# Fused attention and gated convolution on one core: transposes that take turns between two pairs of PSUM banks, a first scores step of its own, and a re-dealt instruction order

## The chip, the cores and the metric

The kernel runs on one core of a Trainium2 chip. The metric is device microseconds of one execution; three runs of the kernel before gave 257.99, 259.13 and 259.63 us, median 259.13 us. The engines are named as the profile names them: PE is TensorE (PEld its weight loads), DVE is VectorE, ACT is ScalarE, POOL is GpSimd, SP is SyncE, which issues the loads and stores.

## The reference

Two stages, the second on the first's output. Four batches, eight heads of width 64, 768 positions; local attention over 96 keys plus 8 global keys, with a linear bias per head.

```python
scores = scale * np.matmul(q, k.transpose(0, 1, 3, 2))
scores = np.where(keep, scores + bias, -1000000000.0)
a = np.exp(scores - np.max(scores, axis=-1, keepdims=True))
a = a / (np.sum(a, axis=-1, keepdims=True) + 1e-09)
x = np.matmul(a, v)                      # all heads side by side: 512 columns
for k in range(5):
    gate_pre += conv_w[k] * xp[:, k:k + S, :]
gate = 1.0 / (1.0 + np.exp(-gate_pre))
out = (gate * (x @ w_val)) @ w_out
```

## The kernel before

**Tiling.** Attention goes by 32 groups (batch, half of the sequence, pair of heads), each of three steps of 128 queries: 96 steps. The second stage goes by eight phases (batch, half), each fed by four groups.

**Operations.** Every operation has a key. For a group g: `L` and `LV` are its loads (SP; group 0's keys and queries come in two parts, `L` 0 and `LB`); `S` all its scores (PE); per step and head `AM` adds the bias and takes the row minimum (DVE), `EX` is the exponential (ACT), `NM` the division by the row sum (POOL, DVE or ACT), with `RG` and `RC` as the guarded reciprocal of a batch of one to three steps; `PT` transposes a batch's probabilities into PSUM (PE), `EV` copies that out in two halves (ACT or DVE), `PV` is the product with the values for a pair of groups (PE), `XS` copies its result out (ACT or DVE). In the second stage `XH` and `XL` split x into a high and a low part, `CV` are the five taps of the convolution, `SG` the tanh, `VM` the product with w_val, `GM` the gate, `GH` and `GL` the split of its result, `OM` the product with w_out, `OE` and `ST` the copy-out and store. `W…` operations decode the 64-bit weights in the first quarter, `BIAS`, `BI2` and `DIST` make the bias tables. `FA`, `FB` and `FC` compute a flag at the end (DVE, PE, DVE).

**Order.** `Plan.add` collects the operations with what each needs; the table `SLOTS` gives each one its place in one list over all engines, and `ENGINES` says which engine does it. The program is emitted in that order, so each engine does its part of the list strictly in order. `plan.ring` adds the dependencies of a buffer that is used in turn.

**PSUM.** Eight banks: two (`pts`) for the transposes, and for the weight sums `WS`; two (`x`) for P.V; two (`s`) for scores; two (`moe`) for `VM` and `OM`. Each `PT` writes both banks of `pts`, so it waits for both `EV` of the `PT` before it.

**Zero products.** `WARM` at the start is 12 products of constants of 512 columns (two of them write `pts`), ahead of the first scores; three blocks `F` of 4, 7 and 6 more stand between the first operations of PE.

Of the kernel before, what the change touches and what calls it, by code (L numbers as in the profile page):

```python
# [16 lines left out]
WARM, FILL_N = 10, (4, 7, 6)  # L17
# [105 lines left out]
    "XH": (
        182, 221, 276, 281, 404, 405, 545, 546, 628, 637, 673, 712, 770, 817, 893, 937, 955, 1010, 1040, 1145, 1164,
        1219, 1249, 1278, 1321, 1361, 1427, 1451, 1509, 1539, 1581, 1608,
    ),
    "XL": (
        191, 229, 284, 285, 468, 538, 554, 569, 647, 766, 767, 780, 826, 850, 962, 965, 989, 1039, 1094, 1175, 1188,
        1222, 1258, 1287, 1325, 1366, 1473, 1477, 1529, 1544, 1597, 1610,
    ),  # L130
# [1042 lines left out]
```

## Time and profile before

| | us |
|---|---|
| median of three runs (lowest, highest) | 259.13 (257.99, 259.63) |
| profiled execution, its own time | 258.13 |
| its span in the trace | 256.3 |
| PE busy | 246.5 |
| DVE busy | 222.4 |
| ACT busy | 193.7 |
| POOL busy | 138.7 |

The span is the time from the first to the last instruction that the profile shows; the time of the same execution is 1.8 us longer. A busy share is a union of instruction times over the whole span; it mixes stretches in which different engines set the pace, so it has to be read stretch by stretch. The end of a matmul is modelled, so PE reads as busy where it only follows closely; what counts for it are the starts of its instructions and the waits listed in front of them.

### The profile page before, as it was taken

The numbers are of one execution on the slowest core, as the hardware profiler recorded it, in microseconds if no ns is written. First come the engines' busy times: TensorE is split into PE (matmuls) and PEld (weight loads), VectorE is DVE, ScalarE is ACT, GpSimd is POOL, SyncE is SP. The second block draws the span as 40 slices with busy tenths as digits, with TensorE's granted clock in tenths as the row PEclk, the third lists the DMA queues.
The fourth block names the chain that finished last, engine by engine and source line by source line (L and its number), as shares of the span: only waits on it lengthen the run. The fifth ranks groups of instructions, "written<-read, shape, count | busy, mean of one in ns | idle before, by whom it ended". The sixth has DMA issues, their size and how long they took to land.

```text
span 256.3 us, 8977 instructions
## 1 busy us (share of the span) xinstructions
PE 246.5 (96%) x3386; PEld 207.5 (81%) x3386; DVE 222.4 (87%) x780; ACT 193.7 (76%) x660; POOL 138.7 (54%) x226
## 2 busy tenths in 40 slices
PE   8989899999999999999999999999999999999983
PEld 3557578788789987999888988898889889889963
DVE  3999999999999999999999889899797797889520
ACT  4989999999989999999897585698966756324011
POOL 4776999999877834344555696154725223140100
PEclk9999999999999999999999999999999999999999
DMA  5969765953256049160628170082012061002112
GB/s 158 379 188 344 245 245 191 391 203 130 63 180 243 17 124 338 56 208 5 226 68 315 69 258 1 8 279 106 6 41 82 4 207 41 0 3 75 47 43 90
DMA packets 16303, 36.37 MB, mean 142 GB/s; under 512 B 1920, under 2 KB 4480, under 8 KB 16256
## 3 DMA queue, kind: packets, MB, share of 16 engines
q1 hardware_dynamic: 16112, 35.75, 40.5%
q8 instruction: 28, 0.46, 0.7%
q14 instruction: 19, 0.16, 0.2%
q10 hardware_dynamic: 144, 0.00, 0.0%
HBM read 29.46 MB, written 6.29 MB: 139 GB/s over the span
## 4 chain that ended last, share of the span: by engine, by line
PE 69%; DVE 21%; ACT 3%; DMA 2%; issue 2%; POOL 1%; SPq 0%; POOLq 0%; DVEq 0%
PE o L859 25%; PE val L836 21%; PE s L624 8%; PE x L709 6%; DVE gate L794 6%; DVE t L632 5%; PE pt L675 5%; PE x L702 3%; DMA kq<-in_kq 2%; ACT p L643 2%; PE warm L406 1%; DVE p L662 1%; DVE ab L299 1%; DVE g L843 1%; DVE rs L654 1%
## 5 line engine op out<-in xcount | busy, mean ns | idle before, releaser
L643 ACT ACTIVATE p<-t,mins 128x168 f32<-128x168 f32 (+1 forms) x192 | 81.2, 427 | 7.8 <-DVE mins L632 3.6
L794 DVE SCALAR_TENSOR_TENSOR gate<-xs,cwt,gate 128x384 f32<-128x384 f32 x128 | 83.0, 664 | 0.8 <-POOL gate L798 0.3
L662 POOL TENSOR_SCALAR p<-p,rs 128x168 f32<-128x168 f32 (+1 forms) x91 | 52.4, 585 | 31.0 <-DVE rs L654 25.3
L632 DVE CUSTOM_DVE_ANT_0 t<-s,bias 128x168 f32<-128x168 f32 (+1 forms) x192 | 54.4, 316 | 3.8 <-PE s L624 3.3
L836 PE MATMUL val<-xh,wvh 128*128 128x384 f32 x128 | 44.9, 351 | 0.5 <-DVE g L843 0.3
L836 PE MATMUL val<-xl,wvh 128*128 128x384 f32 x128 | 43.3, 339 | 0.1
L836 PE MATMUL val<-xh,wvl 128*128 128x384 f32 x128 | 43.2, 338 | 0.0
L850 POOL TENSOR_TENSOR gl<-g,gh 128x384 fp32r<-128x384 f32 x22 | 24.6, 1123 | 29.2 <-DVE gh L299 22.3
L859 PE MATMUL o<-woh,gh 128*128 128x512 f32 (+1 forms) x100 | 40.1, 401 | 0.0
L859 PE MATMUL o<-woh,gl 128*128 128x512 f32 (+1 forms) x100 | 38.6, 386 | 0.9 <-DVE gl L850 0.9
L297 ACT COPY ab<-pt 128x384 f32<-128x384 f32 (+3 forms) x60 | 29.2, 500 | 12.8 <-PE pt L675 12.6
L859 PE MATMUL o<-wol,gh 128*128 128x512 f32 (+1 forms) x100 | 38.6, 386 | 0.0
L624 PEld LDWEIGHTS s<-kq 64*64 64x64 f32 x1088 | 30.9, 133 | 8.6 <-issue 5.6
L643 ACT ACTIVATION_READ_ACCUMULATOR p<-t,mins 128x1 f32 x192 | 37.3, 194 | 0.0
L624 PE MATMUL s<-kq 64*64 64x104 f32 (+3 forms) x1088 | 35.7, 264 | 1.3 <-PE pt L675 0.6
L660 ACT ACTIVATE p<-p,rs 128x168 f32<-128x168 f32 (+1 forms) x68 | 27.9, 428 | 5.2 <-DVE rs L654 5.0
L675 PEld LDWEIGHTS pt<-ident,p 64*104 64x104 f32 (+1 forms) x544 | 19.5, 131 | 9.9 <-issue 3.3
L675 PE MATMUL pt<-ident,p 64*104 64x64 f32 (+1 forms) x544 | 25.3, 226 | 1.8 <-ACT ab L297 1.7
L650 POOL TENSOR_SCALAR sm<-sm 128x4 f32<-128x4 f32 (+2 forms) x31 | 9.2, 296 | 31.2 <-ACT p L643 30.1
L836 PEld LDWEIGHTS val<-xh,wvh 128*128 128x128 f32 x128 | 24.0, 188 | 2.5 <-DVE g L843 0.6
L871 ACT ACTIVATE ob<-o 128x512 f32<-128x512 f32 (+1 forms) x22 | 12.5, 574 | 17.2 <-PE o L859 17.2
L836 PEld LDWEIGHTS val<-xl,wvh 128*128 128x128 f32 x128 | 24.1, 188 | 1.0 <-DVE xl L786 0.3
(157 smaller groups left out, 422.8 us busy)
## 6 DMA issues: line engine op xcount, KB each, us to landing
kq<-in_kq SPq DMA_DIRECT2D x16, 444.0 KB, 5.5
va<-in_va SPq DMA_DIRECT2D x16, 384.0 KB, 4.3
out<-ob SPq DMA_DIRECT2D x24, 256.0 KB, 3.4
kq<-in_kq SPq DMA_DIRECT2D x15, 392.0 KB, 5.7
va<-in_va SPq DMA_DIRECT2D x16, 320.0 KB, 4.5
w<-in_wv SPq DMA_DIRECT2D x8, 256.0 KB, 5.0
w<-in_wo SPq DMA_DIRECT2D x3, 512.0 KB, 4.3
w<-in_wo SPq DMA_DIRECT2D x2, 256.0 KB, 3.5
```

The costliest lines, as they stand in the source:

```text
L297: nc.scalar.copy(dst, src)
L624: nc.tensor.matmul(s[rows, u : u + w], T["rq", g][r, k * P + half * QH : k * P + (half + 1) * QH], T["rk", g][r, c : c + w], start=True, s ...
L632: nc.vector.tensor_tensor_reduce(out=t[:, :n], in0=T["s", s // HB, s % HB, j][:, :n], in1=bias[:, h, :P] if n == P else bias[:, h, P:], op ...
L643: nc.scalar.activation(T["p", s][:, j, :n], T["t", s, j][:, :n], AF.Exp, bias=mins[:, s, j : j + 1], scale=-1.0, accum_out=T["sm", batch_o ...
L660: nc.scalar.mul(pr, pr, rs)
L662: engine(e).tensor_scalar(out=pr, in0=pr, scalar1=rs, scalar2=1.0, op0=ALU.mult, op1=ALU.mult)
L675: nc.tensor.transpose(pts[h][:m, c0 : c0 + QH], pr[rows, c : c + m], ident[rows, rows])
L709: nc.tensor.matmul(T["x", g][rows(i), c0 : c0 + P], T["near", g][:n, k, j], T["a", HB * g + k][:n, j * P : (j + 1) * P], start=False, stop ...
L794: nc.vector.scalar_tensor_tensor(out=gt, in0=src, scalar=w, in1=gt, op0=ALU.mult, op1=ALU.add)
L836: nc.tensor.matmul(T["val", ph, m], (wvh, wvh, wvl)[r][:, m, c * P : (c + 1) * P], (T["xh", g], T["xl", g], T["xh", g])[r], start=(c == 0 ...
L850: engine(e).tensor_sub(tile_of(("gl", ph, m), [P, HT], F32R, "gl", 5), T["g", ph, m], T["gh", ph, m])
L859: nc.tensor.matmul(T[key][:, cols], (T["gh", ph, c], T["gl", ph, c], T["gh", ph, c])[r][:, rows], (woh, woh, wol)[r][:, c, cols], start=(c ...
```

## The change

Four things are changed.

1. The two banks of P.V become fixed tiles `xb`. Within each pair of groups the batches of transposes take turns: the first uses `pts`, the next `xb`, and so on (17 of the 42 batches use `xb`). A `PT` in `xb` needs the `EV` of the earlier `xb` batches of its pair, and the `XS` of the two groups of the pair before.
2. The first step's scores are an operation of their own, `S0`, which needs only the first part of group 0's load; `S` 0 does the other two steps.
3. `WARM` is seven zero products (four of them write the four banks) in place of twelve. The blocks `F` keep their sizes.
4. All places in `SLOTS` and many engines in `ENGINES` are dealt anew.

```diff
-WARM, FILL_N = 10, (4, 7, 6)
+WARM, FILL_N = 3, (4, 7, 6)
...
+    "S0": (8,),
...
-    pts = [psum.tile([P, 4 * P], F32, tag=f"pt{i}", name=f"pt{i}", bufs=1) for i in range(2)]
+    pts, xb = ([psum.tile([P, 4 * P], F32, tag=f"{t}{i}", name=f"{t}{i}", bufs=1) for i in range(2)] for t in ("pt", "x"))
...
+    turns = {}
+    for s in batches:
+        before = [t for t in batches if t // (2 * HB) == s // (2 * HB) and t < s]
+        turns[s] = xb if len(before) % 2 else pts
...
-        for t in (pts if first else []) + [T["warm",]] * n:
+        for t in (pts + xb if first else []) + [T["warm",]] * n:
...
-    def scores(g):
+    def scores(g, ks):
...
-        for k in range(HB):
+        if 0 in ks:
+            for j in range(2):
+                tile_of(("sb", g, j), [P, 4 * P], F32, "s", S_B, psum)
+        for k in ks:
...
-                    nc.tensor.transpose(pts[h][:m, c0 : c0 + QH], pr[rows, c : c + m], ident[rows, rows])
+                    nc.tensor.transpose(to[h][:m, c0 : c0 + QH], pr[rows, c : c + m], ident[rows, rows])
...
-            tile_of(("x", g), [P, HT], F32, "x", X_B, psum)
+            T["x", g] = xb[g % X_B][:, :HT]
...
+    plan.add(("S0",), (PE,), lambda e: scores(0, range(1)), [("L", 0)])
...
-                bank = [d for h in range(2) for d in plan.ring(f"pt{h}", 1, key, [("EV", ss[0], h)])]
+                if turns[s0 := ss[0]] is pts:
+                    bank = [d for h in range(2) for d in plan.ring(f"pt{h}", 1, key, [("EV", s0, h)])]
+                else:
+                    q = s0 // (2 * HB)
+                    bank = [("EV", t, h) for t in batches if t // (2 * HB) == q and t < s0 and turns[t] is xb
+                            for h in range(2)] + [("XS", i) for i in (2 * q - 2, 2 * q - 1) if i >= 0]
```

The new order at three places, read from the two tables:

- PE at the start. Before: `WARM` (12), `S` 0, `F` (4), `S` 1, `PT` 0, `F` (6), `S` 2. After: `WARM` (7), `S0`, `S` 0, `F` (6), `S` 1, `PT` 1, `F` (4), `PT` 0, `S` 2. DVE after `DIST` 1: before two `BIAS`, then the six `AM` of group 0; after one `AM`, one `BIAS`, five `AM`.
- Ahead of `S` 12 (place 477 before, 476 after, with the same operations of PE ahead of it). DVE has 3 `EV`, 2 `XL`, one `BIAS`, `NM`, `RC` and `W2` less, and 2 `GL`, one `GH`, `WH` and `WP` more. POOL has 6 `NM`, 3 `HI`, 2 `BIAS`, one `WA` and `XL` more, and 5 `WH`, one `WP`, `GL` and `RG` less. ACT has 6 `NM`, 2 `EX`, one `BIAS`, `WA` and `XH` less, and 4 `WH`, 3 `EV` and one `GH` more.
- The end. Before, PE: `OM` 84, 85, `FB`, 86, 87, 88, 89; DVE: `GM` 31, `FC`, `GL` 31. After, PE: `OM` 84, 85, `FB`, 86, 88, 89, 87; DVE: `GM` 31, `FC`, with `GL` 31 on POOL. Four taps of group 31 (`CV` 156 to 159) move to a place between `GM` 28 and `GM` 29. Numbers of `OM` count the products of one row block and one quarter of w_out: 84 to 87 are one output block, 88 to 91 the next.

## Rows read from the trace of the kernel before

**Rows 1.** The chain that ended last, by engine (page).

```profile
PE 69%; DVE 21%; ACT 3%; DMA 2%; issue 2%; POOL 1%; SPq 0%; POOLq 0%; DVEq 0%
```

**Rows 2.** Stretches of the span: busy us (x instructions) per engine, granted clock, DMA.

```profile
25.00:60.00 35.00, 33.00 (x614) 27.00 (x606) 34.67 (x132) 34.68 (x124) 33.45 (x49) 1.00 0.69 247
...
92.00:243.60 151.60, 151.52 (x1880) 132.77 (x1877) 134.17 (x422) 107.14 (x348) 64.46 (x96) 1.00 0.32 108
```

**Rows 3.** The chain in order of time near 120 us: start, length, what.

```profile
121.07 0.62 PE pt L675 x16
121.69 1.04 PE s L624 x24
122.73 2.30 PE o L859 x9
```

**Rows 4.** What the transposes (L675) waited for, whole span: us, times.

```profile
  ACT ab L297: 3.3, 6
```

**Rows 5.** Timeline of the first 10 us.

```profile
0.75 1.32 SPq L381 DMA_DIRECT2D kq<-in_kq  x2
...
0.79 1.01 PE L406 MATMUL pt<-const-bfloat16-1.0 128*128 128x512 bf16 x2 [0.79 <-PEq L1163]
1.59 3.84 PE L406 MATMUL warm<-const-bfloat16-1.0 128*128 128x512 bf16 x10
...
5.36 1.02 PE L624 MATMUL s<-kq 64*64 64x128 f32 x32
...
5.56 0.23 DVE L454 TENSOR_SCALAR xs<-xs,counts 128x8 f32<-128x8 f32 x1
...
6.59 0.29 DVE L632 CUSTOM_DVE_ANT_0 t<-s,bias 128x128 f32<-128x128 f32 x1 [0.51 <-PE s L624]
...
7.96 1.31 PE L624 MATMUL s<-kq 64*64 64x128 f32 x32 [0.61 <-DVE mins L632]
...
9.52 1.48 PE L406 MATMUL warm<-const-bfloat16-1.0 128*128 128x512 bf16 x6
```

**Rows 6.** Loads of the first 20 us: issues, KB each, us to landing.

```profile
kq<-in_kq SPq DMA_DIRECT2D x1, 272.0 KB, 3.4
...
kq<-in_kq SPq DMA_DIRECT2D x1, 128.0 KB, 3.1
```

**Rows 7.** Groups by line and shape: busy us, mean ns, idle before.

```profile
L299 DVE COPY ab<-pt 128x384 f32<-128x384 f32 x15 | 8.2, 544 | 0.2 <-PE pt L675 0.2
...
L786 DVE TENSOR_TENSOR xl<-xs,xh 128x384 fp32r<-128x384 f32 x17 | 10.2, 602 | 0.0
...
L850 DVE TENSOR_TENSOR gl<-g,gh 128x384 fp32r<-128x384 f32 x10 | 6.2, 630 | 1.2 <-ACT gh L297 1.2
...
L662 POOL TENSOR_SCALAR p<-p,rs 128x168 f32<-128x168 f32 x74 | 44.1, 603 | 28.5 <-DVE rs L654 23.9 <-ACT p L643 1.8 <-DVE xs L299 1.4
...
L850 POOL TENSOR_TENSOR gl<-g,gh 128x384 fp32r<-128x384 f32 x22 | 24.6, 1123 | 29.2 <-DVE gh L299 22.3 <-ACT gh L297 6.9
...
L299 POOL CAST wvh<-('w', 3)_h 128x512 fp32r<-128x512 f32 x1 | 0.8, 811 | 0.0
...
L299 POOL COPY xs<-xs 128x4 f32<-128x4 f32 x6 | 2.5, 418 | 0.1
...
L297 ACT COPY xs<-x 128x384 f32<-128x384 f32 x26 | 11.9, 468 | 1.7 <-PE x L709 1.7
...
L794 DVE SCALAR_TENSOR_TENSOR gate<-xs,cwt,gate 128x384 f32<-128x384 f32 x128 | 83.0, 664 | 0.8 <-POOL gate L798 0.3
```

**Rows 8.** Timeline of the end.

```profile
243.07 0.51 ACT L297 CAST gh<-g 128x384 fp32r<-128x384 f32 x1 [6.46 <-DVE g L843]
...
244.45 0.39 PE L859 MATMUL o<-woh,gh 128*128 128x512 f32 x1
...
245.11 0.54 DVE L850 TENSOR_TENSOR gl<-g,gh 128x384 fp32r<-128x384 f32 x1
245.70 0.51 PE L859 MATMUL o<-woh,gl 128*128 128x512 f32 x1 [0.86 <-DVE gl L850]
```

More of the change, by code (lines that the diff above doesn't have):

```diff
@@ L25 @@
     "L": (
-        1, 4, 6, 14, 23, 105, 129, 183, 189, 194, 321, 326, 332, 379, 431, 449, 485, 618, 720, 729, 732, 736, 769,
-        825, 935, 1011, 1019, 1024, 1053, 1125, 1229, 1237,
+        1, 4, 6, 11, 26, 105, 140, 186, 190, 198, 263, 303, 348, 359, 440, 502, 506, 600, 616, 638, 685, 716, 770,
+        818, 937, 941, 965, 1004, 1041, 1121, 1138, 1229,
     ),
@@ L30 @@
     "LV": (
-        28, 95, 101, 133, 137, 199, 204, 305, 311, 316, 352, 355, 426, 561, 566, 571, 614, 622, 715, 773, 837, 842,
-        928, 931, 1004, 1056, 1109, 1114, 1226, 1233, 1485, 1498,
+        32, 100, 137, 182, 194, 203, 208, 213, 250, 299, 343, 362, 432, 435, 498, 510, 590, 595, 702, 821, 831, 834,
+        926, 929, 1017, 1021, 1113, 1143, 1239, 1241, 1301, 1342,
     ),
     "WARM": (2,),
-    "F": (21, 78, 52),
+    "F": (58, 79, 24),
     "IOTA": (0,),
-    "UNITS": (16,),
+    "UNITS": (20,),
@@ L38 @@
     "CNT": (7,),
-    "DIST": (9, 12),
-    "BIAS": (18, 20, 15, 19, 17, 25, 13, 22),
[10 rows of a table removed]
-    "CWL": (11,),
-    "CWA": (97,),
-    "CW": (134,),
+    "DIST": (10, 12),
+    "BIAS": (15, 22, 18, 25, 16, 23, 13, 36),
[10 rows of a table added]
+    "CWL": (14,),
+    "CWA": (113,),
+    "CW": (136,),
+    "S0": (8,),
     "S": (
-        10, 39, 67, 106, 136, 173, 217, 264, 294, 350, 399, 442, 477, 511, 541, 594, 648, 693, 762, 818, 867, 905,
-        932, 987, 1046, 1092, 1144, 1209, 1292, 1313, 1355, 1436,
+        17, 41, 72, 107, 139, 175, 217, 259, 302, 347, 402, 439, 476, 511, 570, 630, 678, 706, 763, 810, 863, 903,
+        961, 997, 1035, 1087, 1131, 1222, 1281, 1300, 1389, 1448,
@@ L57 @@
     ),
[1 row of a table removed]
[1 row of a table added]
     "AM": (
[10 rows of a table removed]
[10 rows of a table added]
     ),
     "EX": (
[10 rows of a table removed]
[10 rows of a table added]
     ),
     "RG": (
-        36, 43, 66, 81, 114, 152, 185, 215, 235, 263, 303, 322, 367, 415, 472, 513, 536, 581, 580, 621, 653, 684,
-        746, 791, 839, 875, 909, 960, 969, 1000, 1037, 1070, 1102, 1166, 1256, 1284, 1334, 1348, 1369, 1406, 1475,
-        1517,
+        39, 44, 56, 77, 110, 143, 197, 221, 242, 273, 306, 321, 376, 415, 483, 515, 554, 577, 597, 642, 700, 704,
+        743, 784, 838, 908, 916, 943, 995, 1011, 1055, 1088, 1135, 1171, 1243, 1303, 1333, 1368, 1410, 1447, 1498,
+        1496,
@@ L87 @@
     ),
     "RC": (
-        37, 47, 70, 87, 127, 156, 196, 226, 241, 269, 309, 327, 376, 419, 474, 517, 553, 584, 585, 625, 656, 716,
-        748, 795, 854, 882, 911, 970, 971, 1020, 1048, 1087, 1103, 1173, 1263, 1285, 1350, 1373, 1374, 1409, 1491,
-        1531,
+        42, 46, 57, 85, 115, 147, 206, 226, 261, 283, 327, 329, 384, 419, 490, 520, 559, 585, 611, 649, 711, 713,
+        765, 794, 843, 917, 921, 950, 1006, 1059, 1082, 1091, 1140, 1182, 1244, 1306, 1341, 1374, 1415, 1450, 1508,
+        1512,
@@ L109 @@
+        1586,
     ),
     "EV": (
[5 rows of a table removed]
-    ),
-    "WS": (91, 140, 208, 255),
-    "ZH": (45,),
[5 rows of a table added]
+    ),
+    "WS": (93, 125, 191, 266),
+    "ZH": (19,),
     "XS": (
-        168, 172, 262, 259, 394, 388, 470, 461, 573, 539, 661, 694, 740, 789, 836, 904, 927, 951, 1005, 1043, 1159,
-        1158, 1244, 1275, 1318, 1332, 1384, 1393, 1501, 1516, 1579, 1594,
+        171, 172, 253, 252, 345, 364, 433, 449, 519, 516, 599, 601, 754, 734, 837, 853, 948, 945, 1024, 1037, 1115,
+        1114, 1259, 1240, 1322, 1358, 1417, 1428, 1515, 1540, 1597, 1604,
@@ L122 @@
     ),
     "XH": (
[L124 to L125 removed]
+        173, 200, 271, 288, 351, 542, 543, 567, 606, 686, 695, 786, 826, 828, 867, 898, 1002, 1074, 1097, 1119,
+        1125, 1192, 1269, 1274, 1329, 1367, 1426, 1497, 1519, 1548, 1600, 1608,
     ),
     "XL": (
[L128 removed]
@@ L129 @@
-        1222, 1258, 1287, 1325, 1366, 1473, 1477, 1529, 1544, 1597, 1610,
+        184, 215, 280, 296, 534, 547, 555, 583, 631, 690, 761, 790, 830, 871, 901, 922, 1044, 1089, 1126, 1127,
+        1175, 1235, 1275, 1313, 1376, 1396, 1462, 1513, 1523, 1552, 1611, 1615,
     ),
     "CV": (
[9 rows of a table removed]
[9 rows of a table added]
     ),
-    "HI": (220, 515, 593, 605, 772, 699, 703, 704, 1049, 1131, 1196, 1133, 1419, 1522, 1469, 1587),
+    "HI": (373, 354, 472, 474, 708, 643, 684, 889, 1063, 1072, 1276, 1321, 1438, 1429, 1425, 1459),
@@ L158 @@
-        1407, 1433, 1446, 1459, 1532, 1551, 1562, 1577, 1626, 1633, 1642, 1648,
+        346, 350, 442, 450, 633, 650, 705, 709, 832, 865, 905, 907, 1045, 1083, 1092, 1134, 1219, 1233, 1278, 1310,
+        1383, 1416, 1436, 1451, 1530, 1543, 1560, 1567, 1624, 1635, 1639, 1649,
     ),
     "GH": (
-        366, 393, 480, 500, 667, 689, 713, 731, 880, 890, 936, 939, 1101, 1112, 1127, 1146, 1259, 1266, 1298, 1306,
-        1421, 1441, 1449, 1463, 1540, 1554, 1569, 1580, 1635, 1636, 1644, 1651,
+        353, 414, 467, 470, 655, 664, 712, 723, 849, 887, 914, 942, 1052, 1093, 1095, 1137, 1236, 1263, 1284, 1315,
@@ L163 @@
+        1385, 1422, 1441, 1452, 1534, 1547, 1563, 1573, 1627, 1637, 1643, 1652,
     ),
     "GL": (
-        372, 407, 483, 510, 674, 709, 721, 735, 884, 899, 940, 949, 1110, 1120, 1141, 1150, 1265, 1273, 1302, 1310,
-        1431, 1445, 1452, 1467, 1543, 1557, 1572, 1584, 1638, 1640, 1646, 1653,
+        420, 422, 473, 517, 662, 673, 719, 730, 879, 891, 940, 946, 1066, 1100, 1132, 1157, 1262, 1279, 1287, 1320,
+        1390, 1440, 1449, 1467, 1538, 1551, 1565, 1574, 1642, 1645, 1646, 1654,
     ),
@@ L184 @@
-    "FA": (1620,),
-    "FB": (1650,),
-    "FC": (1652,),
+        620, 610, 605, 773, 762, 933, 1049, 1046, 1117, 1251, 1246, 1204, 1339, 1379, 1375, 1531, 1507, 1527, 1585,
+        1591, 1620, 1668, 1666, 1675,
+    ),
+    "FA": (1580,),
+    "FB": (1651,),
+    "FC": (1653,),
 }
 ENGINES = {
-    "BIAS": "SGSVVGSS",
-    "BI2": "VG",
-    "WA": "GGGGGGSG",
-    "WZ": "GGVGVGGG",
-    "WH": "GGGGSGGS",
+    "BIAS": "SSSVGGGG",
+    "BI2": "GV",
+    "WA": "GGGGGGGG",
+    "WZ": "VVGGGGGG",
@@ L194 @@
+    "WH": "GSSVSSSS",
     "WD": "VVGV",
-    "WP": "GVVVSSSS",
-    "RG": "GVGGGGGGGGGGGGGGGVGVGGGGGGVGVVGGGVGVVVGGGV",
+    "WP": "VVGVSSSS",
+    "RG": "GVGGGGGGGGGGGGVGVGVGVGGGVGGGVGGGVGGVVGVGVG",
     "NM": (
-        "VGGSGSGGVSGSSGGSVGVGVGSGGSGSGSGSGGGSGGGSGSGVGSSGSVGGSSSGSGSGGGSGGSGVVGSGGGVSSGVGVGGSGSGSSGSSVSSS"
-        "GSGSGSGGGSVVVGSVVVSSGSGGSSGGGSVGSSGSSGGGGGGVGGVGGVGSGSSGVGGGGSSVVSVGGSSVGGVGVVGSSSGSSSGGSVSGGGSV"
-    ),
-    "EV": "VSSVSSSSSVSSVSSVSSSVSSSSVSSSSSSVVSSVSSSSSSSSSSSSSSVVSSVSSVVVSSVSSSSVVSSSVSSVSSVSVSSV",
@@ L202 @@
-    "XS": "SSSSSSSSSSSSSSVSSSVSSSVSVSSVSSSV",
-    "XH": "VSSGSGGVSGVVSSSSSSSSSSVVVGGSVVVV",
-    "XL": "VVVGVGVGGVGVVGVVGGGVVGGVGGVGVGVV",
+        "SGGVGGGGGVGSSGGGGGSGGGVGGSGSGGGSGGVGGSGVGSSGGGSSGGSGSGVGSGSGSGGSSGVGGVGVGSGGVGSGSSGGSGGVSSSGVSVS"
+        "GSSVSVSGGVVSGGSGSSSGGGGGGSSSVSSVSVSVSSVVGGSVGSSGSVGSGSSSGVSSSVSGGGVSGGGGSVVVGGGGSSGVSSGSSVVSSSSS"
+    ),
+    "EV": "SSSSSSSSSVVSSSVSSSSSVSSSSSSSSSVSSSSSSSSSSVSSSSVSSSSSSSSSVSSVSSSVVSVSVSVSSSSSVSVVSSSS",
+    "XS": "SSSSSSSSSSVSSSSVSSSVSVSSSSSSSSSV",
@@ L205 @@
+    "XH": "VSSGGSGSGSSVSSGGSVGVSSVSSSVSGSGG",
+    "XL": "GVVGGGVGGGGGGGVVGGGVGVVGVVGVVGVV",
     "CV": (
-        "GVVVVGVVVVSVVVVSVVVVVVVVVGVVVVGVVVVSVVVVGVVVVVVVVVGVVVVVVVVVSVVVVSVVVVGVVVVGVVVVSVVVVVVVVVSVVVVG"
-        "VVVVVVVVVGVVVVSVVVVVVVVVGVVVVGVVVVSVVVVSVVVVSVVVVSVVVVGVVVVVVVVV"
-    ),
-    "HI": "GGGSSSVVVGVGVSVG",
-    "GH": "SVSSSSSSVSVVSSVSSSSSVSSSSSVSVVVS",
-    "GL": "GGGVGGGVGVGGGGGGGGGGGGVVVVGGVVGV",
-    "OE": "VSSSSSSSVSSSSSSSSVSSSSSSS",
+        "GVVVVSVVVVSVVVVGVVVVSVVVVSVVVVGVVVVSVVVVGVVVVGVVVVSVVVVGVVVVGVVVVGVVVVVVVVVSVVVVSVVVVGVVVVGVVVVG"
+        "VVVVGVVVVSVVVVGVVVVGVVVVSVVVVGVVVVSVVVVGVVVVSVVVVGVVVVGVVVVSVVVV"
+    ),
@@ L213 @@
+    "HI": "GGGGVVSVVSGGGVGG",
+    "GH": "VSSVSSSSVVSSVSVSSSSSSVSSSVSSSSSS",
+    "GL": "VGVVGVGVGGVVVGGVGGGVVGGVGVGGVVGG",
+    "OE": "VVSSVSVVSSVSVSSSVSSVSSSSS",
 }
@@ L411, in attention_moe @@
     plan.add(("WARM",), (PE,), lambda e: zeros(WARM))
-    for i in range(HB):
+    for i in range(len(FILL_N)):
         plan.add(("F", i), (PE,), lambda e, i=i: zeros(FILL_N[i]), [("S", 0), ("WARM",)])
@@ L555, in w_low @@
         engine(e).tensor_add(low, h, T[("w", i), "r"])
-    plan.ring("moe", 2, ("WARM",), [("WARM",)] + [("F", s) for s in range(HB)])
+    plan.ring("moe", 2, ("WARM",), [("WARM",)] + [("F", s) for s in range(len(FILL_N))])
     for i in range(2 * NC):
@@ L603, in attention_moe @@
     plan.add(("CW",), (DVE,), taps2, [("CWA",)])
-    def scores(g):
+    def scores(g, ks):
         hf = groups[g][1]
-        banks = [tile_of(("s", g, j), [P, 4 * P], F32, "s", S_B, psum) for j in range(2)]
-        for k in range(HB):
+        if 0 in ks:
+            for j in range(2):
+                tile_of(("sb", g, j), [P, 4 * P], F32, "s", S_B, psum)
+        for k in ks:
             n = width(3 * g + k)
@@ L621, in scores @@
                 r = slice(i * D, (i + 1) * D)
-                s = T["s", g, k, j] = banks[j][:, k * SW : (k + 1) * SW]
+                s = T["s", g, k, j] = T["sb", g, j][:, k * SW : (k + 1) * SW]
                 rows = slice(half * QH, (half + 1) * QH)
@@ L667, in transpose @@
     def transpose(ss):
-        c0 = 0
+        c0, to = 0, turns[ss[0]]
         for s in ss:
@@ L685, in evac_pt @@
                 b += blocks(s)
-        copy(e, T["ab", ss[0]][:, :n, h], pts[h][:, : n * QH].rearrange("p (b q) -> p b q", q=QH))
+        copy(e, T["ab", ss[0]][:, :n, h], turns[ss[0]][h][:, : n * QH].rearrange("p (b q) -> p b q", q=QH))
     def pv(gs):
@@ L712, in s_deps @@
     def s_deps(g):
-        deps = [("L", g)] + ([] if g else [("LB", 0)])
+        deps = [("L", g)] + ([] if g else [("LB", 0), ("S0",)])
         return deps + ([("AM", 3 * (g - 1) + k, j) for k in range(HB) for j in range(2)] if g else [])
@@ L719, in pv_deps @@
         return deps + [d for d in bank if d[0] != "PV" or g == NGRP - 1]
+    plan.add(("S0",), (PE,), lambda e: scores(0, range(1)), [("L", 0)])
     for g in range(NGRP):
-        plan.add(("S", g), (PE,), lambda e, g=g: scores(g), s_deps(g))
+        plan.add(("S", g), (PE,), lambda e, g=g: scores(g, range(0 if g else 1, HB)), s_deps(g))
     for gs in [(g, g + 1) for g in range(0, NGRP - 2, 2)] + [(NGRP - 2,), (NGRP - 1,)]:
@@ L735, in attention_moe @@
                 plan.add(key, (DVE,), lambda e, s=s, j=j: add_bias(s, j),
-                         [("S", g), bias_key(2 * groups[g][2] + head_at(groups[g][2], j), int(full))]
+                         [("S", g) if s else ("S0",), bias_key(2 * groups[g][2] + head_at(groups[g][2], j), int(full))]
                          + plan.ring("t", T_B, key, [("EX", s, j)]))
```

16 lines of the change are left out of this document (6 added, 10 removed), and 136 rows, old and new, of the table SLOTS.

## The prediction

> **What bounds the kernel now.** I began with the chain that ended last: PE holds 69% of it, DVE 21%, ACT 3% [rows 1]. Two engines share it, so the next view is the busy time by stretch [rows 2]. From 25 to 60 us nobody has room: DVE is busy 34.67 of 35 us, ACT 34.68, POOL 33.45, and PE, with 33.0, is the one that waits. From 92 to 243.6 us PE is busy 151.52 of 151.6 us and the chain runs through PE alone, block after block, of which three are shown [rows 3], while DVE has 17 us idle. So the kernel has two regimes. In the front, PE waits for what DVE, ACT and POOL deliver, in the order of their lists; behind it PE has a fixed amount of work and never stops; and at the end there is one hole. Four numbers can change the time: how late the front makes PE, PE's own work, the hole, and the store behind it.
>
> PE's own work is the same in both kernels: the products, scores, transposes and zero blocks `F` keep their number and shape. Only five zero products go, and they stand ahead of the first scores.
>
> **Transposes in turn.** Before, a `PT` waits for the copies of the one before it. In the whole trace this cost 3.3 us in six waits [rows 4], a gross figure: in the front PE is late anyway for DVE, and time saved at one transpose is waited for at the next. In the long PE stretch, with 0.08 us idle, there is almost nothing to remove. So I cost the turn itself at 0; its gain can only come through the lists. Ends: a gain of 3.3 us if each wait was on the path; a loss, which is a rival below. It adds a wait: a `PT` in `xb` stands behind both `XS` of the pair before, and behind it in PE's queue stands everything else.
>
> **The start.** The zero products run from 0.79 to 5.36 us, and the first scores follow at 5.36 at once; DVE, whose last distance table ends at 5.56 + 0.23 = 5.79, does two biases and then waits 0.51 us for the scores, until 6.59 [rows 5]. With seven products PE is free at 0.79 + 7 x 0.38 = 3.5 us at their mean pace (4.57 / 12 = 0.38). `S0` needs the first part of the load, 128 KB: issued at 0.75 [rows 5], landed 3.1 us later [rows 6], so 3.9 us. The second part, issued 1.32 / 2 = 0.7 us behind, lands 3.4 us later, at about 4.8, and the other 24 of the 32 score products take 24/32 x 1.02 = 0.77 us, to 5.6. `AM` 0 can therefore start at 5.79, when DVE is ready, not at 6.59. The six `AM` of group 0 have ended when `S` 1 starts, at 7.96 [rows 5]: 1.37 us from the first to that point. Add one bias, about 0.2 us: 5.79 + 1.37 + 0.2 = 7.36. The gain at this point is 0.6 us; ends 0 (the load lands later than its median) and 0.8 us (the bias hidden).
>
> **The lists of the front.** Ahead of `S` 12 both orders hold the same PE work, so what the others must do before it can be counted from the two tables. DVE: three copies of `ab` at 0.544 and two `XL` at 0.602 less, two `GL` at 0.630 more [rows 7], -1.63 - 1.20 + 1.26 = -1.6 us; four small operations less against three more I take at nought. With the start, DVE could be 2.2 us earlier. ACT has six divisions less and four casts and three copies more and comes out no heavier. POOL: six divisions at 0.603 and three history copies at 0.418 more, five casts at 0.811 (the dearest) less: +3.6 + 1.3 - 4.1 = +0.8 us; its two more biases lie ahead of 25 us, and its other five single changes I take at nought. POOL had 35 - 33.45 = 1.55 us idle between 25 and 60 us [rows 2], so it can follow DVE by only 1.55 - 0.8 = 0.75 us before it is the one that is late. The front ends 0.75 us (POOL) to 2.2 us (DVE) earlier; I take 1.2, nearer to POOL. From that point PE never waits in the trace of before, so a microsecond here is one at the end.
>
> **The loads.** The places of `L`, `LV` and `WL` shift by a few operations of the list. Most are issued earlier against their use; one, `LV` 3, comes later, behind the weight load `WL` 4. I cost them at 0; the loads' landing times of 3 to 4 us [rows 6] bound what one that is late could cost.
>
> **The end.** PE starts a product at 244.45 and the next at 245.70. They stand 0.23 us apart in an unbroken stretch (2.30 us for nine and one switch, [rows 3]), so PE is 1.0 us late [rows 8]. It waits for `GL` 31, which DVE does only behind the flag `FC`, at 245.11, though its input `GH` 31 was ready at 243.07 + 0.51 = 243.58. After, `GL` 31 is on POOL, with 1.12 us for one [rows 7]: ready at 244.7, and ahead of the product that needs it PE now has `OM` 88 and 89, six more products or 1.4 us. The hole goes: -1.0 us. What is late next is the last store, as before. What could take its place: the four taps of group 31 stand between `GM` 28 and `GM` 29, 4 x 0.664 = 2.7 us of DVE [rows 7], in which PE goes on with `VM` products of the next quarter; I see them just covered, and bound the loss at 0.6 us.
>
> **Sum.** -1.2 (front) - 1.0 (end) = -2.2 us. The profiled execution took 258.13 us; it would take 255.9. The median of the runs is 259.13, 1.0 above that execution, and I set the same difference against it: **256.9 us**.
>
> **Rivals.**
>
> *DVE alone sets the front.* POOL's wait is absorbed because its divisions are needed later than the list says. Then the front gives 2.2 and the sum is -3.2: 255.9. For it: DVE has 21% of the chain, POOL 1% [rows 1]. Against: 33.45 of 35.
>
> [...]
>
> *POOL eats the front.* It has the six extra divisions, and DVE only waits sooner: the front gives nothing, the end 1.0: 258.1.
>
> *Nothing arrives.* The order is only different, and the end finds another hole: 259.1.
>
> *The shared bank stalls PE (slower).* Fifteen of the 17 `PT` in `xb` wait for `XS`. ACT does most of these, at 0.468 us [rows 7], in the order of a queue that was full [rows 2]. Where it is one copy late, PE loses that with all that is behind it. The gain of 2.2 us is used up at 0.15 us a time, the kernel is 1% slower at 0.32, and at a full copy each it is 256.9 + 7.0 = 263.9 us. Against: in the new list these `PT` mostly stand three or more us of PE work behind that `PV`, say a transpose block, a scores block and some `OM` of 0.62 + 1.04 + 2.30 us [rows 3], and two copies take 0.94. Only the first, 1.7 us behind, is close.
>
> **How the numbers follow.** Forecast 0.36 (256.9, itself between 256.0 and 258.0), DVE alone 0.20, slow array 0.14, POOL 0.12, nothing 0.07, shared bank 0.11. Three runs of the kernel spread over 1.6 us, so about 1% (2.6 us) is what a measurement can tell from no change: faster means under 256.5. That is DVE alone and under half of the forecast, 0.20 + 0.17 = 0.37. Slower, over 261.7, is the most of the shared bank, 0.10; the rest, 0.53, is within 1%. The range 254.6 to 259.8 reaches from 1.3 below the DVE case (gross bank waits that were on the path after all) to past nothing, and leaves the stall out.
>
> **What would show it.** Right: `AM` 0 at about 5.8 us and `S` 1 at about 7.4; PE without waits from a point some 1.2 us earlier against the same operations; in that front POOL at over 34 of 35 us; transposes waiting on `ab` under 1 us in all; no hole before `OM` 87. Wrong: score products at twice their time near 5 us; waits of PE on `xs` copies or of `PV` on `va`; a wait of `VM` on `GM` 29 near the end; any idle time of PE between 92 and 240 us, which would upset the view that a shorter front is all gain.

## The result, and the profile after

The changed kernel takes 255.16 us in the median of six runs (254.61 to 256.06); the kernel before, beside it, 259.00 (257.99 to 259.63). The ratio is 0.986, 95% interval 0.983 to 0.989: 3.8 us less, with an interval from 2.9 to 4.4. The profiled execution took 255.96 us with a span of 254.2, against 258.13 and 256.3: 2.2 less, the sum that was forecast. That agreement is partly chance, as the stretches show.

The chain that ended last, by engine, of the kernel after:

```profile
PE 85%; ACT 5%; DVE 3%; POOL 2%; issue 1%; DMA 1%; ACTq 0%; POOLq 0%; DVEq 0%
```

DVE's share has fallen from 21% to 3% [rows 1]. The stretches of the kernel after (busy us and instructions of PE, PEld, DVE, ACT, POOL; granted clock; DMA):

```profile
25.00:60.00 35.00, 32.93 (x568) 26.75 (x567) 34.00 (x129) 33.43 (x118) 32.50 (x48) 1.00 0.76 260
60.00:92.00 32.00, 31.79 (x550) 27.24 (x551) 31.40 (x123) 30.76 (x111) 23.22 (x35) 1.00 0.51 168
92.00:241.00 149.00, 149.00 (x1892) 131.04 (x1882) 131.09 (x413) 109.90 (x359) 60.30 (x95) 1.00 0.31 100
```

In this execution all three helpers are less full than in [rows 2], POOL at 32.50 and not over 34, and PE is busy no longer than it was. But the execution holds a stop of PE that the same list doesn't always have (1.26 us at 33.6, below). The same stretch of e9, whose list is that of the kernel after up to `S` 15:

```profile
25.00:60.00 35.00, 34.41 (x585) 27.66 (x583) 34.91 (x137) 34.33 (x120) 33.51 (x49) 1.00 0.78 273
```

Without the stop the helpers are as full as before, and PE is busy 34.41 of 35 us (34.10 in e3, 34.40 in e4) where it was busy 33.00. From 92 us on PE is busy without a gap, as before. What PE waited for, in the whole span:

```profile
PE x L709 <- ACT ab L298: 1.3, 2, 0.8
PE pt L682 <- issue: 1.3, 1, 1.3
PE sb L631 <- DMA kq<-in_kq: 1.1, 2, 0.8
```

No transpose waits for copies of `ab` now; the waits on those copies have moved to P.V. In the trace of before, the same view has

```profile
PE pt L675 <- ACT ab L297: 1.7, 3, 0.9
```

which is half of [rows 4]: that row counts each of three waits twice, once for the product and once for its weight load. New are one stop of 1.3 us for which the profile shows no engine ("issue"), and the scores' wait for their loads. The first 10 us after:

```profile
3.86 0.61 PE L631 MATMUL sb<-kq 64*64 64x128 f32 x8
...
4.79 0.82 PE L631 MATMUL sb<-kq 64*64 64x168 f32 x24 [0.33 <-DMA kq<-in_kq]
...
5.54 1.48 PE L411 MATMUL warm<-const-bfloat16-1.0 128*128 128x512 bf16 x6
...
5.80 0.29 DVE L639 CUSTOM_DVE_ANT_0 t<-sb,bias 128x128 f32<-128x128 f32 x1
...
7.84 1.14 PE L631 MATMUL sb<-kq 64*64 64x128 f32 x32 [0.82 <-DMA kq<-in_kq]
```

`AM` 0 starts at 5.80, within a hundredth of where the working put it, but `S` 1 only at 7.84, not 7.4: it waits 0.82 us for group 1's load, which nobody had waited for before [rows 5]. The end after:

```profile
242.40 0.48 PE L872 MATMUL o<-woh,gh 128*128 128x512 f32 x1
...
242.46 1.01 POOL L863 TENSOR_TENSOR gl<-g,gh 128x384 fp32r<-128x384 f32 x1 [1.12 <-ACT gh L298]
...
242.72 0.40 PE L872 MATMUL o<-woh,gl 128*128 128x512 f32 x1
```

`GL` 31 is done by POOL at 243.5, while PE goes on with `OM` 88 and 89; the hole of [rows 8] is gone, and no `VM` waits for `GM` 29.

Where the time went is best read at three points of PE that have the same work ahead of them in either order: the start of `S` 12, the first product of `OM` 84 and the last product. From the traces, those of the next section's experiments included (us):

| kernel | `S` 12 | `S` 12 to `OM` 84 | `OM` 84 to last product |
|---|---|---|---|
| before | 61.83 | 180.40 | 9.60 |
| after | 62.01 | 178.96 | 8.47 |
| e1, end alone | 61.63 | 180.27 | 8.48 |
| e2, turns alone | 63.93 | 180.26 | 9.59 |
| e5, less DVE | 62.63 | 180.29 | 9.60 |
| e6, less POOL | 62.55 | 180.32 | 9.60 |
| e7, less ACT | 63.20 | 180.27 | 9.60 |
| e10, end and block `F` | 63.03 | 180.39 | 8.48 |
| e11, less of all | 62.81 | 180.41 | 9.59 |
| e3, after without its end | 60.97 | 179.01 | 9.59 |
| e4, after with 12 zero products | 61.48 | 178.96 | 8.47 |
| e12, after with other loads | 62.79 | 178.99 | 8.47 |
| e9, after with pairs parted | 60.95 | 181.72 | 8.47 |

The second and third column repeat within 0.15 us for an order; the first scatters by up to 2.3. So in the two profiled executions the front gave nothing (+0.2), the long stretch, where PE "never waits", gave 1.44, the end 1.13, and the last store gave 0.3 back (2.6 us from issue to landing, before 2.3).

### The profile page after: what moved, and what is told of

Same layout as the page of the kernel before. It is cut to its first block, busy times and chain, and to the rows that moved or that the text cites. A ratio compares the mean times of both kernels' runs of the same rounds, so it can differ in the third digit from the quotient of the medians.

```text
span 254.2 us, 8955 instructions
## 1 busy us (share of the span) xinstructions
PE 244.3 (96%) x3381; PEld 206.1 (81%) x3381; DVE 218.3 (86%) x768; ACT 197.3 (78%) x670; POOL 136.2 (54%) x228
## 4 chain that ended last, share of the span: by engine, by line
PE 85%; ACT 5%; DVE 3%; POOL 2%; issue 1%; DMA 1%; ACTq 0%; POOLq 0%; DVEq 0%
PE val L849 27%; PE o L872 26%; PE sb L631 10%; PE x L716 9%; PE x L709 5%; PE pt L682 4%; ACT p L650 3%; PE x L682 3%; POOL p L669 1%; DMA counts_i<-in_counts 1%; ACT ab L298 1%; PE pt L544 1%; DVE t L639 1%; POOL sm L657 1%; DVE ob L886 1%
## 5 line engine op out<-in xcount | busy, mean ns | idle before, releaser
L639 DVE CUSTOM_DVE_ANT_0 t<-sb,bias 128x168 f32<-128x168 f32 (+1 forms) x192 | 54.5, 315 | 5.0 <-PE sb L631 4.9
L669 POOL TENSOR_SCALAR p<-p,rs 128x168 f32<-128x168 f32 (+1 forms) x86 | 49.7, 589 | 14.9 <-ACT p L650 5.7
L631 PEld LDWEIGHTS sb<-kq 64*64 64x64 f32 x1088 | 30.9, 134 | 10.5 <-issue 7.1
L631 PE MATMUL sb<-kq 64*64 64x104 f32 (+3 forms) x1088 | 36.1, 265 | 1.2 <-DMA kq<-in_kq 1.1
L667 ACT ACTIVATE p<-p,rs 128x168 f32<-128x168 f32 (+1 forms) x72 | 28.8, 428 | 3.8 <-DVE rs L661 3.7
L863 POOL TENSOR_TENSOR gl<-g,gh 128x384 fp32r<-128x384 f32 x17 | 18.5, 1091 | 16.1 <-ACT gh L298 15.7
L799 POOL TENSOR_TENSOR xl<-xs,xh 128x384 fp32r<-128x384 f32 x18 | 20.2, 1120 | 9.3 <-ACT xh L298 7.8
L716 PE MATMUL x<-ab,va 104*64 104x128 f32 (+1 forms) x384 | 24.7, 277 | 0.0
L298 ACT COPY ab<-pt 128x384 f32<-128x384 f32 (+3 forms) x41 | 19.4, 481 | 6.1 <-PE pt L682 6.1
L849 PEld LDWEIGHTS val<-xh,wvl 128*128 128x128 f32 x128 | 24.1, 188 | 0.0
```

The lines of the kernel that those rows point to most:

```text
L298: nc.scalar.copy(dst, src)
L631: nc.tensor.matmul(s[rows, u : u + w], T["rq", g][r, k * P + half * QH : k * P + (half + 1) * QH], T["rk", g][r, c : c + w], start=True, s ...
L639: nc.vector.tensor_tensor_reduce(out=t[:, :n], in0=T["s", s // HB, s % HB, j][:, :n], in1=bias[:, h, :P] if n == P else bias[:, h, P:], op ...
L667: nc.scalar.mul(pr, pr, rs)
L669: engine(e).tensor_scalar(out=pr, in0=pr, scalar1=rs, scalar2=1.0, op0=ALU.mult, op1=ALU.mult)
L716: nc.tensor.matmul(T["x", g][rows(i), c0 : c0 + P], T["near", g][:n, k, j], T["a", HB * g + k][:n, j * P : (j + 1) * P], start=False, stop ...
```

## The experiments

In the texts on record, letters name the theories of that run alone.

**e1: the end alone,** in the kernel before.

```diff
-    "GL": "...V",   # 31
+    "GL": "...G",
-  OM 86, 87, 88, 89
+  OM 86, 88, 89, 87
```

> The kernel before with only the change of the end: GL 31 on POOL and OM 88 and 89 ahead of OM 87. Theory A (the end is a part of its own, worth the hole): 1.0 us less than the kernel before, no idle time of PE ahead of OM 87, from the first OM 84 to the last product 8.5 us as after, not 9.6. Rival B (the hole only moves to the store, or the new order needs the rest of the list): within 0.3 us of before.

258.99 us against 258.66 for before, ratio 1.0009 (0.9989 to 1.0029): no gain, so theory A fell as it stood. Yet the hole is gone, and PE needs 8.48 us, not 9.60, from `OM` 84 on. It is lost behind the last copy. The DMA view of before, from just before the last store is issued to the span's end:

```profile
q1 hardware_dynamic: 144, 0.26, 18.3%
q14 instruction: 2, 0.02, 1.0%
issues: line engine op xcount, KB each, median us to landing
out<-ob SPq DMA_DIRECT2D x1, 256.0 KB, 2.3
```

and of e1:

```profile
q1 hardware_dynamic: 156, 0.28, 14.4%
q8 instruction: 1, 0.02, 1.6%
q14 instruction: 2, 0.02, 0.8%
issues: line engine op xcount, KB each, median us to landing
out<-ob SPq DMA_DIRECT2D x1, 256.0 KB, 3.8
```

The store took 1.5 us longer, and a packet of 16 KB of the queue "instruction" (q8) lies in its time. Before has 28 such packets in the trace, the last at 252.03, shortly ahead of its last store's first packet; the earlier store of e1 runs into it. Nine of that store's packets start only at 253.59, where the q8 packet, begun at 252.19, ends; all others had ended by 252.9. e10 tests whether the time follows.

**e2: the turns alone,** in the list of before.

```diff
+    TURNS = (1, 3, 9, 14, 86, 92)
+    turns = {t: xb if t in TURNS else pts for t in batches}
...
-                    nc.tensor.transpose(pts[h][:m, ...
+                    nc.tensor.transpose(to[h][:m, ...
```

> The kernel before, its list untouched, with the banks taken in turn wherever that list allows it: batches 1, 3, 5, 7, 37 and 40 go to the P.V banks, among them the two transposes that waited longest (0.54 us at 17.55, 0.89 at 26.66) and the weight sum that waited 0.33 at 28.40. Twelve zero products as before. Theory A (the waits on copies are not on the path, DVE, ACT and POOL set the front): the three waits fall away or turn into waits on something else, and the time stays within 0.3 us of before. Rival B (the turn itself gives the gain): 1.4 to 1.8 us less, and PE reaches the end of the front that much earlier.

259.65 us, ratio 1.0035 (1.0017 to 1.0053): not faster, a little slower. What PE waited for in e2:

```profile
PE x L677 <- DVE p L664: 0.8, 1, 0.8
...
PE x L677 <- POOL p L664: 0.8, 1, 0.8
...
PE pt L677 <- ACT ab L297: 0.4, 1, 0.4
```

The two waits on the copies, 0.54 and 0.89 us, have become waits on the divisions `p` of 0.8 us each, at the same two transposes. At these two places of the old list a free bank gains nothing. e2's scores also began 0.55 us late (5.91 us, before 5.36); whether the turns cost the rest of its 1 us is left open.

**e3: the changed kernel with its end put back.**

```diff
-    "GL": "...G",   # 31
+    "GL": "...V",
-  OM 86, 88, 89, 87
+  OM 86, 87, 88, 89
```

> The changed kernel with the end put back: GL 31 on DVE behind the flag, OM 87 ahead of 88 and 89. Theory A: 1.0 to 1.1 us more than the changed kernel (some 2.7 less than before), with the hole ahead of OM 87 back. Rival B (the end is worth nothing): equal to the changed kernel.

255.90 us, ratio 0.9912 (0.9879 to 0.9944), where the changed kernel has 0.986: 0.7 us more by the medians, 1.3 by the ratios. The hole is back (9.59). Theory A holds here: in the changed kernel the end is worth what it says.

**e4: twelve zero products** in the changed kernel.

```diff
-WARM, FILL_N = 3, (4, 7, 6)
+WARM, FILL_N = 8, (4, 7, 6)
```

> The changed kernel with twelve zero products again. Theory A (S 1 waits for its load in any case, so the earlier start is worth little): S0 at 5.4, AM 0 at 6.0, S 1 at 7.9 to 8.2, and 0.1 to 0.4 us more than the changed kernel. Rival B (the start is worth what the prediction gave it): 0.6 us more or above. Rival C (more zero products make the array faster from the first scores on): no loss or a gain.

255.6 us, ratio 0.9877 (0.9850 to 0.9904), 0.4 us over the changed kernel, with intervals that overlap (0.983 to 0.989). The traces are clearer: against e3, which has seven, `S0` starts at 5.44 (3.90), `S` 1 at 8.20 (7.77) and `OM` 84 at 240.44 (239.98): 1.54 us at the first scores, of which 0.43 to 0.51 is left from `S` 1 on. That is just over theory A's range and under B's; C fell.

**e5, e6, e7: less work for one engine** in the front of the kernel before.

```diff
     def conv(e, g, k):                       # e5
+        if (g, k) in ((1, 2), (2, 1), (3, 1)):
+            return
     def norm(e, s, j):                       # e6; e7: (19, 1), (20, 1), (22, 1), (26, 1)
+        if (s, j) in ((19, 0), (20, 0), (25, 0)):
+            return
```

> The kernel before with three taps of the convolution left out on DVE in the front (group 1 tap 2, group 2 tap 1, group 3 tap 1), 3 x 0.664 = 2.0 us of DVE ahead of S 12. Theory A (DVE alone sets the front, and POOL's wait is absorbed): PE reaches OM 84 1.5 to 2.0 us earlier and the time falls by as much. Rival B (POOL, at 33.45 of 35 us, is next, as the forecast took it): at most 0.75 us. Rival C (ACT, at 34.68 of 35, is as full as DVE): 0 to 0.4 us.

> The kernel before with three divisions left out on POOL in the front (step 19, 20 and 25, one head each), 3 x 0.603 = 1.8 us of POOL. Theory A (DVE): within 0.4 us of before. Rival B (POOL shares the limit): 0.8 us or more less. Both can't be had from POOL alone if DVE is at 34.67 of 35.

> The kernel before with four divisions left out on ACT in the front (steps 19, 20, 22 and 26, one head each), 4 x 0.433 = 1.7 us of ACT. Theory A (DVE): within 0.4 us of before. Rival C (ACT is the limit, whose copies the transposes and P.V wait for): 1.0 us or more less.

258.75, 259.08 and 258.47 us; ratios 1.0007 (0.9987 to 1.0027), 1.0021 (1.0002 to 1.0040), 0.9994 (0.9978 to 1.0010). None gains, and `S` 12 comes at 62.55 to 63.20, no earlier than in before (61.83) and e1 (61.63). All three single-engine theories fall, the one of the forecast among them. e11 takes all three away.

**e11: all of it at once.**

> The kernel before with what the three runs before left out, all at once: three taps on DVE, three divisions on POOL, four on ACT, 2.0, 1.8 and 1.7 us. Theory H (the three engines limit the front together, and relief for one leaves PE to the other two): 1.2 to 2.0 us less than before, most of it by S 9. Rival I (the front is set by the order of the lists and by PE's own blocks and changes, not by the amount of work): under 0.6 us less.

258.36 us, ratio 0.9993 (0.9969 to 1.0018). The front of e11:

```profile
25.00:60.00 35.00, 32.99 (x629) 26.70 (x630) 34.05 (x128) 33.48 (x119) 30.14 (x48) 1.00 0.70 252
```

POOL has 4.9 us idle now, ACT 1.5, DVE 1.0, and PE is busy as long as in [rows 2] (32.99 us). Rival I. The front of the old list is not set by the amount of the helpers' work; 5.5 us less of it changes nothing that can be told from the noise.

**e8: the changed kernel without turns,** its list kept as far as that goes.

```diff
-        turns[s] = xb if len(before) % 2 else pts
+        turns[s] = pts
...
-            assert all(self.ops[self.at[d]][0] < slot for d in deps), ...
+        for _ in range(200):
+            for i, op in enumerate(self.ops):
+                at[i] = max([at[self.at[d]] + 0.01 for d in op[3]] + [at[i]])
```

> The changed kernel with all transposes in their own two banks again, its list kept but for the places that this forbids: a transpose that stood ahead of the copies of the one before is moved to just behind them, and what needs it behind that. Theory A (the gain is the division of the work in the lists, and the turns are worth nothing): 0 to 0.6 us more than the changed kernel, which is over 2.5 below before. Rival D (the turns are what lets the new list keep PE fed): 1.5 us more or above, with the waits on the copies of ab back in the front.

277.49 us, ratio 1.0736 (1.0689 to 1.0783). Rival D, far beyond its size. Two of its stretches and its waits:

```profile
10.00:25.00 15.00, 11.11 (x169) 7.96 (x163) 10.49 (x55) 10.35 (x49) 8.18 (x17) 0.89 0.68 224
...
92.00:260.00 168.00, 162.68 (x2077) 139.35 (x2068) 138.69 (x450) 118.81 (x392) 65.55 (x103) 0.99 0.32 103
```

```profile
PE pt L684 <- ACT ab L300: 2.5, 4, 1.1
PE val L851 <- ACT ob L886: 1.9, 1, 1.9
```

Transposes wait on copies again, and PE stands still even behind 92 us, for 5.3 us. So the new list can't be had without the turns, while the turns are worth nothing in the old one (e2). The 22 us are no price of a bank, though: many operations were pushed back, 512 columns took 0.46 us at the start here and not 0.25 (see the rivals below), and not every part of it is taken apart.

**e9: pairs of transposes parted.** In the new list eleven pairs of `PT` stand side by side on PE, in the old one pair; this is counted from the two tables. Ten of the eleven lie behind `S` 12; the other, ahead of it, is the pair of the old list. e9 parts nine of the ten. The instructions of DVE, ACT, POOL and SP keep their order.

```diff
-    "PT": ( ... 640, ... 759, ... 873, ... 967, ... 1043, ... 1141, ... 1386, ... 1458, ... 1555, ...
+    "PT": ( ... 644.5, ... 763.5, ... 878.5, ... 969.5, ... 1048.5, ... 1147.5, ... 1389.5, ... 1464.5, ... 1557.5, ...
```

> The changed kernel with nine of its eleven neighbouring pairs of transposes parted again: the second of each goes behind the next block of PE (seven behind a block of VM or OM, two behind scores); banks, division among engines and everything else stay. In the traces so far a change from large to small products costs PE 0.095 us, back 0.149, from one kind of small products to another 0.142. Theory E (turns let two transposes stand side by side, which saves PE these changes, where the prediction held PE's own work for equal): 7 x 0.244 + 2 x 0.142 = 2.0 us more than the changed kernel, with PE still free of waits. Theory A (the lists of DVE, ACT and POOL give the gain): 0 to 0.3 us more.

258.48 us, ratio 0.9997 (0.9975 to 1.0020): the whole gain is gone, 3.3 us by the medians. The traced execution is the fastest of the twelve, and its trace shows 2.7 of them. At `S` 12, `S` 13 and `S` 14 the traces of e9 and e3 stand within 0.02 us (`S` 14 at 73.45 in both); from `S` 12 to `OM` 84 e9 takes 2.7 us more, 0.30 per pair, and no wait of PE is listed between 92 and 240 us. The chain in order of time around one pair, in the kernel after (start, length, what):

```profile
136.86 0.95 PE sb L631 x27
137.81 0.49 PE x L682 x12
138.30 0.35 PE pt L682 x12
138.65 3.50 PE val L849 x19
```

and the same place in e9:

```profile
137.87 0.49 PE x L684 x12
138.35 0.72 PE val L851 x3
139.07 0.48 PE pt L684 x12
139.55 2.45 PE val L851 x13
```

(The window cuts the last piece of each.) Twelve transposes behind other transposes take 0.35 us here, behind anything else 0.48 or 0.49. From the first transpose of this pair to the next transposes on PE, with 24 `VM` products between in either kernel, are 5.20 us in the kernel after (from 137.74) and 5.53 in e9 (from 137.80): 0.33 us for one more change into small products and out of them. In the old list, too, nearly every block of transposes stands alone:

```profile
128.53 0.49 PE pt L675 x12
129.02 1.04 PE s L624 x24
...
131.99 0.49 PE pt L675 x12
132.48 0.90 PE o L859 x3
```

Theory E holds; 2.7 us were measured where 2.0 was expected.

The 1.44 us themselves come out near when the changes are counted, with the intervals of the last section. Between `S` 12 and `OM` 84 the new list has 13 changes from one kind of small products to another less, and one more each way between small and large: 13 x 0.142 - 0.095 - 0.149 = 1.6 us. In the old list 17 of the 28 blocks of transposes in that stretch come behind scores or P.V, other small products; e9 puts seven of nine between large products on both sides, so that parting nine pairs costs more than forming ten had gained.

**e10: the end, with PE's program a little shorter,** in the kernel before.

```diff
-WARM, FILL_N = 10, (4, 7, 6)
+WARM, FILL_N = 10, (0, 7, 6)
...
+  and the edit of e1
```

> The kernel before with the end changed as in the run of the end alone, and the first block F (4 zero products, ahead of S 1, which waits 0.67 us for DVE there) left out, so that PE's program is 8 instructions shorter. The run with the turns alone, of about this length, had 27 loads of 16 KB of PE's instructions and not 28; the 28th lay beside the last store in the run of the end alone, and that store landed 3.35 us after its issue, not 1.78. Theory F (the end is worth 1.1 us, and that load took it back): 27 loads, the last store lands 1.8 to 2.2 us after its issue, and the time is 0.9 to 1.3 us below before. Rival G (stores that follow closer on each other land later, whatever PE loads): it lands over 3 us after its issue, and the time is that of before.

257.73 us, ratio 0.9956 (0.9936 to 0.9977): 0.9 to 1.1 us less, theory F. The block `F` left out gives PE nothing at `S` 1, which starts 2.61 us behind the first scores in e10 and in before; it was not left out alone. There are 27 packets of q8 in its trace, and in the time of the last store none:

```profile
q1 hardware_dynamic: 155, 0.28, 19.6%
q14 instruction: 2, 0.02, 1.1%
issues: line engine op xcount, KB each, median us to landing
out<-ob SPq DMA_DIRECT2D x1, 256.0 KB, 2.4
```

(The figures in the expectation count from the start of the issue to the last packet of data, those of the view to the signal, half a microsecond later.) The kernel after has 27 as well, and 2.6 us for its last store.

**e12: a candidate beyond the changed kernel.**

```diff
-  SP: L 1, WL 0, L 2, WL 1, L 3, CWL
+  SP: L 1, CWL, L 2, WL 0, WL 1, L 3
...
-        plan.add(("ST", ph, k), (SP,), lambda e: store(ph, k), [("OE", ph, k, half) for half in range(2)])
+            plan.add(("ST", ph, k, half), (SP,), lambda e, half=half: store(ph, k, half), [("OE", ph, k, half)])
```

> A candidate beyond the changed kernel, with two edits far apart: the taps' small load and the load of group 2 go ahead of the first weights, so that group 1's load, for which S 1 waited 0.8 us, shares the queues with less; and the last output block is stored in two halves, the first as soon as it is copied. Expected: S 1 at 7.5 us rather than 7.84 and the same 0.3 us at OM 84; the last store, of half the size, 0.3 us sooner to land; together 0.5 us below the changed kernel. Rival: weight decoding or the taps come late (waits on the loads of weights near 10 us), and it is equal or up to 1 us slower.

256.98 us, ratio 0.9908 (0.9876 to 0.9941): 1 us or more slower than the changed kernel, so nothing was won. Its start on PE:

```profile
5.05 1.40 PE L631 MATMUL sb<-kq 64*64 64x168 f32 x24 [0.25 <-DMA kq<-in_kq]
6.39 2.74 PE L411 MATMUL warm<-const-bfloat16-1.0 128*128 128x512 bf16 x6
9.06 1.32 PE L631 MATMUL sb<-kq 64*64 64x128 f32 x32
```

The 24 scores take 1.40 us instead of 0.82 and the six zero products 2.74 instead of 1.48: 0.46 each, where they took 0.25 after. `S` 1 is 1.2 us later for that. The loads are therefore not tested by this run. The two half stores ended no sooner: the last was issued 0.72 us behind the last product as in all kernels, and its last packet came 2.0 us later, with a packet of q8 beside it from 251.02 to 251.90.

## Why the prediction came out, step by step

**The forecast** of 256.9 was 1.7 us high against the median; the 255.9 for the profiled execution was met within 0.1. Start and end were right in kind; 1.4 us of the gain stand where nothing was put.

- *"PE's own work is the same in both kernels"* is the step that failed. The products are the same, their neighbours are not. A block of transposes more cost PE 0.33 us to enter and leave at the place shown for e9, and ten more pairs of transposes side by side save 1.4 us between `S` 12 and `OM` 84, where the prediction had "almost nothing to remove". *"I cost the turn itself at 0; its gain can only come through the lists"* is true to the letter (e2, e8), but the list was searched for DVE's and POOL's work only, not for PE's order. e9 shows it: parting nine pairs takes back 2.7 us.
- *The lists of the front, -1.2 between POOL (0.75) and DVE (2.2).* The ground fell. Busy shares of 96 to 99% [rows 2] were read as a limit, and less work for DVE, POOL, ACT or all of them moves nothing (e5 to e7, e11). Nor are the helpers less full in the new list (e9, e3, e4). The size came near all the same, by luck: from `S` 1 to `S` 12 the traces of e3, e4 and e9 take 53.2 to 53.3 us, those of the old list 53.9 to 54.7 (e2 55.4). What holds PE in the old front is left open: by e11 it is the order and what waits for what, not the amount.
- *The transposes' 3.3 us in six waits* were 1.7 us in three, counted twice [rows 4]. The sum took them at 0 and stays; the end "a gain of 3.3 us if each wait was on the path" should have been 1.7.
- *The start, -0.6 (0 to 0.8).* `AM` 0 came as worked out. PE was free at 3.9 us, not 3.5, because the first zero products start 0.43 us apart and the mean of 0.38 holds the faster last three; the load landed no sooner, so this cost nothing. `S` 1 then met a load that was costed at 0, because no row of before shows a wait on it. Measured to the end of PE's work, five zero products less are worth 0.46 (e4 against e3).
- *The end, -1.0.* 1.13 on PE, 0.7 to 1.3 in the changed kernel by time (e3). That it was an independent term was wrong: in the kernel before it brings nothing (e1), where a packet of q8 lies among those of the last store and the store takes 3.8 us to land, and 1 us where none does and it takes 2.4 (e10). The bound of 0.6 for the taps was not needed.
- *Loads at 0.* 0.82 us of wait at `S` 1.

**Why the median fell by 3.8, the traces by 2.2.** Eight traces of the old order (before, e1, e2, e5, e6, e7, e10, e11) reach `S` 12 at 61.6 to 63.9, median 62.7; the one that was read is 0.9 early. The trace after holds the stop of 1.26 us "issue" at 33.6, which e3 and e9, with the same list there, don't have: they reach `S` 12 at 60.97 and 60.95. Together that is 2.1 us, more than the 1.6 to be explained. By such executions the gain is about 1.7 up to `S` 12, 1.4 to `OM` 84, 1.1 to the last product. Of the 1.7, 0.46 is the start; the rest lies between `S` 1 and `S` 12 and isn't taken apart.

**The rivals.** *DVE alone* gave 255.9 and came nearer than the forecast, by the wrong road. *POOL eats the front* fell: the front gained although POOL was as full as before (33.51 in e9), and relieving it of 1.8 us (e6) changed nothing. *Nothing arrives* and *the shared bank stalls PE* fell; no wait of a transpose on `xs` is among those of the kernel after, and PE is busy 149.00 of 149 us behind 92. *Slow array*, at 0.14 among the chances, with score products at twice their time near 5 us, did not happen in the trace after, where the 24 scores at 4.79 take 0.82 us and the six zero products 0.25 each. It came near in e12 and e8, where the 24 scores take 1.40 us, 1.7 times as long and not twice, and the six zero products 0.46 us each, from 6.39 and 6.55 us on, behind pauses of PE of 0.17 and 0.25 us in e12 and of 0.66 in e8; `S` 1 starts at 9.06 and 9.23 against 7.84, 1.2 to 1.4 us later. The trace after, e3 and e9, with the same seven zero products and pauses of 0.33 to 0.96 us ahead of the 24 scores, had 0.25 us from 5.5 to 6.0 us on, so what decides between the two is open.

## What to carry to other kernels

An engine at 99% in a stretch is not yet its limit: take work from it and see whether the chain moves, and if nothing moves, as here with 5.5 us less on DVE, POOL and ACT (e11), read the order. On a PE that never waits, count the blocks as well as the products: where small products lie between large ones, putting two small blocks of one kind side by side saved 0.14 us here where their neighbours were small too and about 0.3 between large ones, and took a second set of PSUM banks and an order dealt for it. The hole of 1.1 us near the end brought nothing where the store behind it took 3.8 us to land, with a packet of q8 among its own (e1), and about 1 us where it took 2.4, with none (e10), so read the last store's time to landing with such a hole.
